# Joining the halves of a chunk's inverse on four tiles of the array, and planned margins for the router, in a DeltaNet and mixture-of-experts kernel

## The chip, the cores and the metric

The kernel runs on one core of a Trainium2 chip. The core has five engines that work at the same time, each through its own instructions in order: TensorE (PE, matrix products), VectorE (DVE), ScalarE (ACT), GpSimd (POOL) and SyncE (SP, here only for starting DMA transfers). PE reads its operands from the on-chip memory (SBUF) and writes to eight accumulator banks (PSUM). DVE and ACT copy from there. PE's weight loads are listed apart as PEld. The metric is the device time of one execution in microseconds (us): the median of three runs before the change is 909.04 us (907.24 to 909.8).

## What is computed

Two stages, all in fp32. The first is a DeltaNet attention with batch 4, 8 heads, 768 tokens and head size 48. The second sends each of the 3072 tokens to two of eight experts.

```python
for t in range(S):                       # DeltaNet, state is B x H x 48 x 48
    kt, vt, bt = k_n[:, :, t], v[:, :, t], beta[:, :, t, None]
    y[:, :, t] = einsum('bhd,bhde->bhe', q[:, :, t], state)
    v_old = einsum('bhde,bhd->bhe', state, kt)
    state = state + bt[..., None] * einsum('bhd,bhe->bhde', kt, vt - v_old)
x = y.transpose(0, 2, 1, 3).reshape(3072, 384)
logits = x @ w_gate                      # 8 experts
noisy = logits + log1p(exp(x @ w_noise)) * noise
top2, weights = two largest of noisy, softmax over the two
out[token] += weight * (relu(x[token] @ w1[e]) @ w2[e])    # 384 -> 1024 -> 384
```

## The kernel before

**DeltaNet in chunks.** The recurrence is done in chunks of 64 tokens. A *unit* is one chunk of two batch entries with their eight heads: the two entries lie in partitions 0 to 63 and 64 to 127. Two units make a chunk of all four batch entries, and four units (two chunks) make a step `s`. There are six steps. For each step the kernel does, in this order of mention (lines 1220 to 1247):

- `products(n)` for its four units: the keys are turned by PE (`turned`, L484) and copied by ACT (L489), multiplied with themselves (`by_token`, L500), and ACT copies the diagonal blocks of 32x32 into `gd` (L529) and the block below the diagonal into `at` (L535).
- `invert(s)`: DVE inverts 32x32 triangular blocks for all units of the step at once. It transposes `gd` into `t` (L546), takes the keys' lengths with a square root that ACT works out as a logarithm and an exponential (L553, L554), scales `t` with a factor that POOL prepares (`low_d`, L582, then L589), and eliminates 30 columns one after another (L597, L601). At the end it scales (L614) and transposes twice, into `tb` (L622) and `tt` (L628).
- `within(n)`: the queries are turned as the keys are, multiplied with the keys (L500), and DVE multiplies the product with a causal mask into `qk` (L693).
- `join(n)`: each 64x64 inverse is put together from two 32x32 ones. A first product (L646) multiplies `at` with `tb`, ACT negates it into `x` (L653), a second product (L658) multiplies `x` with the lower diagonal block, and ACT copies the result into the inverse `w64` (L665). Four ACT copies place the diagonal blocks (L672). A product is eight heads times two batch entries, each a 32x32x32 matmul on its own 32x32 tile of the PE array; the trace records each as two. The first product of a unit reads the upper and writes the lower rows of both batch entries, the second the other way round. So each stands on two of the array's tiles, and the two together on four. Both products of a unit use the same PSUM bank.
- `recur(n)` and `answer(n)`: the recurrence of the unit (L731, L741, L748, L759, L771), its output, and the router's logits (L814 to L853).
- `route(s)`: some 30 small instructions for the four units: exponential (L895), rounding (L897 to L903), logarithm on ACT (L980), the two largest (L913 to L930), a count of earlier tokens on PE (L935 to L941), row numbers (`r_at`, L948), weights, and POOL's eight scatters of rows to DRAM (L325).

**A planner sets the order.** None of this is issued as written. Each piece is a job with an engine, an estimated cost, the keys it reads and writes, a PSUM bank that it opens, uses or closes, and sometimes a due time. `Jobs.order` (L84) simulates the five engines with these costs, takes for each engine the ready job that is due first, and the jobs are then issued in the order of their planned starts. A job's successor is planned to be ready when the job ends, plus `SIGNAL` (0.15 us) if it stands on another engine, plus `lands`, a delay that until now only transfers have. The hardware keeps only the order: an engine whose next instruction is not ready waits, and with it what is queued behind. Two single PSUM banks and three pairs of banks serve all jobs. Jobs of expert 0 (`early`, rows of the first steps) are marked `late` and fill what is left.

**The experts.** After DeltaNet comes `rest()`, which does the remaining rows of expert 0: two row tiles are turned (L1551), copied into `xe_r` by DVE (L1555), and multiplied (L1562 and on). Experts 1 to 7 follow, with a Strassen-like scheme of seven instead of eight block products. Weights and rows come by SP's transfers, results are added with POOL's gathers and scatters.

Of the kernel before, what the change touches and what calls it, by code (L numbers as in the profile page):

```python
# [16 lines left out]
C = 64  # L17
DP = 64
Q = 32
# [19 lines left out]
class Jobs:  # L39
# [44 lines left out]
    def order(self):  # L84
        jobs = self.jobs
        for job in reversed(jobs):
            for i in job.after:
                jobs[i].due = min(jobs[i].due, job.due - job.cost - self.SIGNAL)
        for job in jobs:
            job.key = (0, job.due) if job.late is None else (1, job.late)  # L90
        waits = [len(job.after) for job in jobs]
        then = [[] for _ in jobs]
        for job in jobs:
            for i in job.after:
                then[i].append(job.number)
# [15 lines left out]

        done = []
        while len(done) < len(jobs):
            first = {}
            best = None
            for engine in self.ENGINES:
                at = []
                for i in could[engine]:
                    start = max(free[engine], ready[i], spaced if jobs[i].apart else 0.0)
                    if jobs[i].opens:  # L120
                        which = jobs[i].opens.size, jobs[i].opens.among
                        if which not in first:
# [12 lines left out]
            could[job.engine].remove(i)  # L135
            end = free[job.engine] = start + job.cost
            if job.apart:
                spaced = start + job.apart
            if job.opens:
                size, among = job.opens.size, job.opens.among  # L140
                job.opens.at = x = first[size, among][1]
                empty[size][x] = None
                job.opens.tile = self.banks[size][x]
            if job.closes:
                empty[job.closes.size][job.closes.at] = end + self.SIGNAL
            job.start = start
            if job.moves:
                end = moved = max(moved, end) + job.moves
            done.append(job)
            for j in then[i]:  # L150
                ready[j] = max(
                    ready[j],
                    end + job.lands + (self.SIGNAL if jobs[j].engine != job.engine else 0.0),
                )
                waits[j] -= 1
                if not waits[j]:
                    could[jobs[j].engine].add(j)
        return sorted(done, key=lambda job: job.start)
# [8 lines left out]
def kernel(  # L167
# [39 lines left out]
    nc = tc.nc  # L207

    B, H, S, D = q.shape
# [6 lines left out]
    US = 2 * NU  # L216
# [59 lines left out]
    before = const.tile([128, E], FP32, name="before")  # L276
# [96 lines left out]
    def deltanet(ictx):  # L373
# [10 lines left out]
        def bank(size, ahead=False):  # L384

            if size == 2:
                return Bank(2, (0, 1) if ahead else (0, 1, 2))
            return Bank(1, (0,) if ahead else (0, 1))
# [85 lines left out]
        def halves(name, slot):  # L474
            return [(name, slot, i) for i in range(2)]

        def turned(n, name, src, size, to, to_size):

            p = bank(1, True)

            def emit():
                p_t = p.tile.rearrange("p (j t) -> p j t", t=128)
                for j in range(NP):
                    nc.tensor.transpose(p_t[:, j], src(n)[:, 2 * j : 2 * j + 2], ident)  # L484

            jobs.add(PE, 0.75, emit, reads=halves(name, n % size), opens=p)
            jobs.add(
                ACT, 0.6,
                lambda: nc.scalar.copy(  # L489
                    to(n), p.tile.rearrange("p (j t) -> p j t", t=128)  # L490
                ),
                writes=[(name + "T", n % to_size)], closes=p,
            )
# [135 lines left out]
                reads=["low_d"], writes=["tt"],  # L629
            )  # L630

        def join(n):

            i = n % US
            at, w64, x = ats(n), w64s(n), xs(n)
            tb, tt = (y[:, i * H : (i + 1) * H] for y in (tbs, tts))
            pairs = [(slice(lo, lo + Q), slice(lo + Q, lo + 2 * Q)) for lo in (0, C)]
            p = bank(1)

            def p_x():  # L640
                return p.tile.rearrange("p (z h i) -> p z h i", z=2, i=Q)

            def first():
                for h in range(H):
                    for up, dn in pairs:
                        nc.tensor.matmul(  # L646
                            p_x()[dn, 0, h], at[up, h % 2, h // 2], tb[up, h],
                            start=(h == 0), stop=(h == H - 1), skip_group_check=True,
                        )

            def negated():
                for up, dn in pairs:
                    nc.scalar.mul(x[dn], p_x()[dn, 0], -1.0)  # L653

            def second():
                for h in range(H):
                    for up, dn in pairs:
                        nc.tensor.matmul(  # L658
                            p_x()[up, 1, h], x[dn, h], w64[dn, h, Q:C],
                            start=(h == 0), stop=(h == H - 1), skip_group_check=True,  # L660
                        )

            def joined():
                for up, dn in pairs:
                    nc.scalar.copy(w64[up, :, Q:C], p_x()[up, 1])  # L665

            w, below = ("w", n % NW), [("w", n % NW, lo) for lo in (Q, C + Q)]
            for lo in range(0, 128, Q):
                rows, cols = slice(lo, lo + Q), slice(lo % C, lo % C + Q)
                jobs.add(  # L670
                    ACT, 0.4,
                    lambda rows=rows, cols=cols: nc.scalar.copy(w64[rows, :, cols], tt[rows]),  # L672
                    reads=["tt"], writes=[("w", n % NW, lo)],
                )
            jobs.add(PE, 1.15, first, reads=["tb", ("at", n % NT_)], opens=p)
            jobs.add(ACT, 0.8, negated, writes=[("x", n % 2)], uses=p)
            jobs.add(PE, 1.15, second, reads=[("x", n % 2), *below], uses=p)
            jobs.add(ACT, 0.8, joined, writes=[w], closes=p)

        def within(n):  # L680

# [4 lines left out]
                lambda: by_token(  # L686
                    two_banks(p, C), kTs(n), lambda z, j, b: qTs(n)[z, j, rows_of[b]]
                ),
                reads=[("kT", n % NT_), ("qT", n % NQ)], opens=p,
            )  # L690
            jobs.add(
                DVE, 0.7,
# [181 lines left out]
        def route(s):  # L874
# [87 lines left out]
            def counted():  # L962
# [12 lines left out]
                ),  # L975
                writes=[("num", s % 2)],
            )
            jobs.add(ACT, 0.5, small_exp, reads=every_logit, writes=["r_u"])
            jobs.add(DVE, 1.0, rounding, reads=["r_u"], writes=["r_w", "r_d", "r_noisy"])
            jobs.add(ACT, 0.25, lambda: nc.scalar.activation(w, w, ACTF.Ln), writes=["r_w"])  # L980
            jobs.add(
                DVE, 0.9, noisy_logits, reads=["r_d", "noise", *every_logit],
# [4 lines left out]
            )  # L987
            jobs.add(
                DVE, 1.7, the_second, reads=["r_noisy", "r_hit0", "r_top0"],
                writes=["r_rest", "r_hit1", "r_p1", "r_taken"],  # L990
            )
            jobs.add(PE, 1.5, count_earlier, reads=["r_taken", "before"], opens=p)
            jobs.add(ACT, 0.25, lambda: nc.scalar.activation(p1, p1, ACTF.Exp), writes=["r_p1"])
            jobs.add(
                DVE, 1.5, rows, reads=["r_hit0", "r_hit1"],
# [224 lines left out]
        for s in range(NS):  # L1220
# [17 lines left out]
            for n in units:  # L1238
                load(n, "q")
                load(n, "v")  # L1240
                within(n)
            for n in units:
                join(n)
            for n in units:
                recur(n)
                answer(n)
# [29 lines left out]
    with ExitStack() as ectx:  # L1276
# [253 lines left out]
        def rest():  # L1530
# [15 lines left out]
            for i, size in enumerate(rows_in[t0:]):  # L1546
# [3 lines left out]
                for do in range(KT):  # L1550
# [1 line left out]
                        p_xt[:, do, 0:size], xr[0:size, i, do * 128 : (do + 1) * 128],  # L1552
                        ident[0:size, 0:size],
                    )
                nc.vector.tensor_copy(  # L1555
                    xe_r[:, :, i * 128 : i * 128 + size], p_xt[:, :, 0:size]
                )
            banks = [*bank_a, *bank_c, *bank_d]
# [219 lines left out]
```

## Time and profile before

The profiled execution has a span of 925.4 us; the three timed runs lie some 16 us below it. The kernel's DeltaNet part ends at about 381 us, expert 0 fills PE to 463 us, and the rest is experts 1 to 7.

| | busy us | share |
|---|---|---|
| PE | 824.5 | 89% |
| DVE | 509.0 | 55% |
| ACT | 310.2 | 34% |
| POOL | 323.7 | 35% |

| group | recorded instructions | busy us |
|---|---|---|
| L646, first product of the join | 768 | 22.4 |
| L658, second product of the join | 768 | 25.3 |
| L672, ACT copies of diagonal blocks | 96 | 38.5 |
| L653 and L665, ACT, around the products | 48 and 48 | 18.0 and 17.4 |
| L693, DVE, masked product | 24 | 16.4 |
| L980, ACT, the router's logarithm | 6 | 1.4 |
| L1555, DVE, rows of `rest()` | 2 | 0.9 |

Busy time is what the instructions of a group took, with overlapping ones counted once. A wait is charged to the instruction that could not start, and to the one that released it; everything behind it on the same engine waits too. A matmul's recorded duration holds its way through the array, so the throughput of many is read from their starts and not from one duration. PE's clock is granted at full or at half speed by stretches, and the page's slices and the rows of a stage show the mean.

### The profile page before, as it was taken

Reading aid. Unit: us, or ns where it says so; the run is one execution under the profiler, and the core shown is the slowest. Engines: PE = TensorE matmul, PEld = TensorE weight load, DVE = VectorE, ACT = ScalarE, POOL = GpSimd, SP = SyncE. Lnnn points to the kernel's source line nnn. Section 1 sums busy time; section 2 is a strip of 40 time slices with the busy share of each in tenths; the row PEclk is TensorE's granted clock in tenths of the full one; section 3 lists DMA queues with packets and bytes.
Section 4 is the critical chain, followed back from the end, with each engine's and each line's share of the span. In section 5 each row is a group of like instructions: output and inputs, shape, how many; then the busy total and the mean of one; then the engine's idle time right before and its main releaser. Section 6 shows DMA issues by size and latency. Waiting matters only on the chain. (4 is left out here: it accounts for less than half of the span.)

```text
span 925.4 us, 21745 instructions
## 1 busy us (share of the span) xinstructions
PE 824.5 (89%) x9170; PEld 639.0 (69%) x9170; DVE 509.0 (55%) x1212; ACT 310.2 (34%) x741; POOL 323.7 (35%) x331
## 2 busy tenths in 40 slices
PE   4678896989879868998899999999999999999995
PEld 3467885867758757655658758759669568578584
DVE  6959888497586971202555435455365354344342
ACT  3564635636348233311133042041140330330410
POOL 3021243332424322132441552552642624615302
PEclk8557686585775955999899999999999999999998
DMA  4698545362413122340441422414314421401201
GB/s 70 117 313 166 101 104 164 89 206 43 134 70 71 55 77 66 141 139 25 158 151 69 142 87 86 160 51 142 129 38 146 134 68 44 129 1 43 65 18 39
DMA packets 119084, 93.76 MB, mean 101 GB/s; under 512 B 84646, under 2 KB 109255, under 8 KB 118976
## 3 DMA queue, kind: packets, MB, share of 16 engines
q1 hardware_dynamic: 107312, 64.54, 25.4%
q0 software_dynamic: 9552, 27.33, 8.7%
q8 instruction: 74, 1.21, 0.6%
q10 hardware_dynamic: 2112, 0.39, 0.3%
q14 instruction: 34, 0.28, 0.1%
HBM read 58.82 MB, written 34.81 MB: 101 GB/s over the span
## 5 line engine op out<-in xcount | busy, mean ns | idle before, releaser
L367 POOL DMA_INDIRECT out_dram<-sums,index x49 | 48.5, 989 | 161.7 <-DVE sums L1267 138.9
L325 POOL DMA_INDIRECT rows_x<-y,slot x48 | 47.3, 986 | 123.5 <-DVE t L601 46.8
L597 DVE TENSOR_TENSOR part<-t 128x30 f32<-128x30 f32 (+9 forms) x180 | 69.1, 384 | 5.3
L1379 PE MATMUL a<-xe,w1e 128*128 128x416 f32 x168 | 69.2, 521 | 0.0
L601 DVE TENSOR_TENSOR t<-t,part 128x30 f32<-128x30 f32 (+9 forms) x180 | 62.9, 349 | 6.2
L358 POOL DMA_INDIRECT sums<-out_dram,index x49 | 51.6, 1054 | 34.3 <-issue 24.9
L1449 ACT COPY part_c<-c 128x416 f32<-128x416 f32 x28 | 14.1, 505 | 120.9 <-PE c L1379 120.6
L484 PE MATMUL single<-ident,kp 128*128 128x128 f32 x96 | 23.3, 388 | 34.0 <-ACT kT L489 16.8
L1379 PEld LDWEIGHTS a<-xe,w1e 128*128 128x128 f32 x168 | 29.6, 189 | 31.4 <-issue 19.2
L784 POOL COPY wide<-st 64x384 f32<-64x384 f32 x44 | 28.6, 651 | 61.4 <-DVE st L771 51.6
L1440 DVE TENSOR_TENSOR hT<-part,d 128x416 f32<-128x416 f32 x28 | 16.4, 587 | 57.8 <-ACT part L1457 56.3
L741 PE MATMUL single<-v,w 64*64 64x48 f32 x768 | 41.5, 278 | 6.1 <-issue 4.0
L1267 DVE SCALAR_TENSOR_TENSOR sums<-d,gate,sums 128x192 f32<-128x192 f32 x56 | 23.4, 417 | 42.4 <-PE d L1379 42.4
L1434 ACT ACTIVATE hT<-hT 128x416 f32<-128x416 f32 x84 | 45.1, 550 | 4.2 <-DVE hT L1440 1.4
L741 PEld LDWEIGHTS single<-v,w 64*64 64x64 f32 x768 | 38.6, 195 | 7.2 <-issue 6.8
L1416 ACT COPY xe<-x 128x384 f32<-128x384 f32 x21 | 10.0, 478 | 100.1 <-PE x L1411 100.1
L484 PEld LDWEIGHTS single<-ident,kp 128*128 128x128 f32 x96 | 15.2, 196 | 39.3 <-issue 16.6
L1379 PE MATMUL d<-xe,w1e 128*128 128x416 f32 x112 | 41.6, 513 | 0.0
L1379 PE MATMUL c<-xe,s_w 128*128 128x416 f32 x112 | 41.4, 512 | 0.0
L1440 DVE TENSOR_TENSOR hT<-part,c 128x416 f32<-128x416 f32 x28 | 16.4, 587 | 41.9 <-ACT part L1468 37.5
L672 ACT COPY w<-tt 32x256 f32<-32x256 f32 x96 | 38.5, 401 | 2.4 <-DVE tt L628 0.7
L1379 PE MATMUL d<-t_w,hT 128*128 128x192 f32 x224 | 38.6, 326 | 0.0
(242 smaller groups left out, 1917.5 us busy)
## 6 DMA issues: line engine op xcount, KB each, us to landing
w1e<-in_moe_w_dram SPq DMA_DIRECT2D x8, 1536.0 KB
w2e<-in_moe_w_dram SPq DMA_DIRECT2D x8, 1536.0 KB
xr<-rows_x SPq DMA_DIRECT2D x7, 1164.0 KB
rows_x<-empty SPq DMA_DIRECT2D x8, 776.0 KB
v<-in_v_dram SPq DMA_DIRECT2D x48, 96.0 KB
qp<-in_q_dram SPq DMA_DIRECT2D x48, 96.0 KB
out_dram<-empty SPq DMA_DIRECT2D x4, 1152.0 KB
kp<-in_k_dram SPq DMA_DIRECT2D x44, 96.0 KB
```

The source lines that it names most:

```text
L325: d = nc.gpsimd.indirect_dma_start(out=rows_x, out_offset=bass.IndirectOffsetOnAxis(ap=slot, axis=0), in_=rows, in_offset=None,).ins
L358: nc.gpsimd.indirect_dma_start(out=got, out_offset=None, in_=out, in_offset=bass.IndirectOffsetOnAxis(ap=index, axis=0), bounds_check=N - ...
L367: nc.gpsimd.indirect_dma_start(out=out, out_offset=bass.IndirectOffsetOnAxis(ap=index, axis=0), in_=got, in_offset=None, bounds_check=N - ...
L484: nc.tensor.transpose(p_t[:, j], src(n)[:, 2 * j : 2 * j + 2], ident)
L597: v_.tensor_tensor(out=part, in0=t_inv[:, j + 1 :, j, None].to_broadcast(shape), in1=t_inv[:, None, j, 0:j].to_broadcast(shape), op=ALU.mult,)
L601: latest["column"] = v_.tensor_tensor(out=t_inv[:, j + 1 :, 0:j], in0=t_inv[:, j + 1 :, 0:j], in1=part, op=ALU.add).ins
L672: lambda rows=rows, cols=cols: nc.scalar.copy(w64[rows, :, cols], tt[rows]),
L741: nc.tensor.matmul(per_head(p_u)[b, h], w64[b, h], v_n[b, h], start=(h == 0), stop=(h == H - 1), skip_group_check=True,)
L784: nc.gpsimd.tensor_copy(wide[rows, :, :, y * D : (y + 1) * D], new[rows])
L1379: nc.tensor.matmul(p, lhsT, rhs, start=opens and i == 0, stop=i == len(products) - 1, skip_group_check=True,)
L1434: relu = lambda m, l, src: nc.scalar.activation(hT[:, m, half[l]], src, ACTF.Relu)
L1440: nc.vector.tensor_tensor(out=hT[:, m, half[l]], in0=x, in1=y, op=ALU.add)
```

## The change

1. `join` takes all units of a step. The four ACT copies of each unit come first in the list. Then there are five blocks of products instead of eight: the first product of unit 0 alone; the second product of unit 0 and the first of unit 1, issued in turn, matmul by matmul; the same for units 1 and 2, and for units 2 and 3; and the second product of unit 3 alone. A mixed block stands on four 32x32 tiles, and its two results lie in the same PSUM bank, in different quarters of the partitions. Each block opens a bank of its own; it is planned at 1.25 us, where each of the eight was planned at 1.15. A block waits for all that its two products read. The number of matmuls and of ACT copies is the same.
2. In the planner, `lands` counts only for successors on another engine.
3. Jobs of compute engines get a `lands`: 2.0 us for the query product whose result DVE masks, and, in all steps but the last, 4.0 for the router's rounding, 4.0 for its second largest, 2.0 for its count.
4. In `rest()` the two copies into `xe_r` are done by ACT.

```diff
-                    end + job.lands + (self.SIGNAL if jobs[j].engine != job.engine else 0.0),
+                    end + (self.SIGNAL + job.lands if jobs[j].engine != job.engine else 0.0),
...
+            for n, m in zip([*units, None], [None, *units]):
+                p = bank(1)
+                reads = []
+                if n is not None:
+                    reads += ["tb", ("at", n % NT_)]
+                if m is not None:
+                    reads += [("x", m % 2), *(("w", m % NW, lo) for lo in (Q, C + Q))]
...
+                def products_of(n=n, m=m, p_x=p_x):
+                    for h in range(H):
+                        for up, dn in pairs:
+                            if n is not None:
+                                nc.tensor.matmul(
+                                    p_x()[dn, h], ats(n)[up, h % 2, h // 2],
+                                    part_of(tbs, n)[up, h], start=(h == 0),
+                                    stop=(h == H - 1), skip_group_check=True,
+                                )
+                            if m is not None:
+                                nc.tensor.matmul(
+                                    p_x()[up, h], xs(m)[dn, h], w64s(m)[dn, h, Q:C],
+                                    start=(h == 0), stop=(h == H - 1),
+                                    skip_group_check=True,
+                                )
...
+                jobs.add(PE, 1.25, products_of, reads=reads, opens=p)
+                if n is not None:
+                    jobs.add(
+                        ACT, 0.8, negated, writes=[("x", n % 2)],
+                        **{"closes" if m is None else "uses": p},
+                    )
+                if m is not None:
+                    jobs.add(ACT, 0.8, joined, writes=[("w", m % NW)], closes=p)
...
-                reads=[("kT", n % NT_), ("qT", n % NQ)], opens=p,
+                reads=[("kT", n % NT_), ("qT", n % NQ)], opens=p, lands=2.0,
...
+            easy = lambda x: x if paced else 0.0
...
+                DVE, 1.0, rounding, reads=["r_u"], writes=["r_w", "r_d", "r_noisy"],
+                lands=easy(4.0),
...
+                writes=["r_rest", "r_hit1", "r_p1", "r_taken"], lands=easy(4.0),
...
+                PE, 1.5, count_earlier, reads=["r_taken", "before"], opens=p, lands=easy(2.0)
...
-            for n in units:
-                join(n)
+            join(list(units))
...
-                nc.vector.tensor_copy(
+                nc.scalar.copy(
                     xe_r[:, :, i * 128 : i * 128 + size], p_xt[:, :, 0:size]
                 )
```

More of the change, by code (lines that the diff above doesn't have):

```diff
@@ L484, in emit @@
                     nc.tensor.transpose(p_t[:, j], src(n)[:, 2 * j : 2 * j + 2], ident)
-            jobs.add(PE, 0.75, emit, reads=halves(name, n % size), opens=p)
+            jobs.add(
+                PE, 0.75, emit, reads=halves(name, n % size), opens=p,
+            )
             jobs.add(
@@ L630, in invert, with join @@
             )
[L632 to L636, printed above, removed]
+        def join(units):
             pairs = [(slice(lo, lo + Q), slice(lo + Q, lo + 2 * Q)) for lo in (0, C)]
[L638 to L644, printed above, removed]
-                    for up, dn in pairs:
[L646 to L656, printed above, removed]
-                    for up, dn in pairs:
[L658 to L678, printed above, removed]
@@ new lines, in part_of @@
+            def part_of(t, n):
+                i = n % US
+                return t[:, i * H : (i + 1) * H]
+            for n in units:
+                w64, tt = w64s(n), part_of(tts, n)
+                for lo in range(0, 128, Q):
+                    rows, cols = slice(lo, lo + Q), slice(lo % C, lo % C + Q)
+                    jobs.add(
+                        ACT, 0.4,
+                        lambda rows=rows, cols=cols, w64=w64, tt=tt: nc.scalar.copy(
+                            w64[rows, :, cols], tt[rows]
+                        ),
+                        reads=["tt"], writes=[("w", n % NW, lo)],
+                    )
@@ new lines, in join, with p_x, negated, joined @@
+            for n, m in zip([*units, None], [None, *units]):
[5 more added lines that the diff above has]
+                    reads += [("x", m % 2), *(("w", m % NW, lo) for lo in (Q, C + Q))]
+                def p_x(p=p):
+                    return p.tile[:, 0 : H * Q].rearrange("p (h i) -> p h i", i=Q)
+                def products_of(n=n, m=m, p_x=p_x):
[12 more added lines that the diff above has]
+                                    skip_group_check=True,
+                                )
+                def negated(n=n, p_x=p_x):
+                    for up, dn in pairs:
+                        nc.scalar.mul(xs(n)[dn], p_x()[dn], -1.0)
+                def joined(m=m, p_x=p_x):
+                    for up, dn in pairs:
+                        nc.scalar.copy(w64s(m)[up, :, Q:C], p_x()[up])
+                jobs.add(PE, 1.25, products_of, reads=reads, opens=p)
+                if n is not None:
+                    jobs.add(
+                        ACT, 0.8, negated, writes=[("x", n % 2)],
+                        **{"closes" if m is None else "uses": p},
+                    )
+                if m is not None:
+                    jobs.add(ACT, 0.8, joined, writes=[("w", m % NW)], closes=p)
@@ L977, in route @@
             )
-            jobs.add(ACT, 0.5, small_exp, reads=every_logit, writes=["r_u"])
-            jobs.add(DVE, 1.0, rounding, reads=["r_u"], writes=["r_w", "r_d", "r_noisy"])
+            easy = lambda x: x if paced else 0.0
+            jobs.add(
+                ACT, 0.5, small_exp, reads=every_logit, writes=["r_u"]
+            )
+            jobs.add(
+                DVE, 1.0, rounding, reads=["r_u"], writes=["r_w", "r_d", "r_noisy"],
+                lands=easy(4.0),
+            )
             jobs.add(ACT, 0.25, lambda: nc.scalar.activation(w, w, ACTF.Ln), writes=["r_w"])
@@ L989, in route @@
                 DVE, 1.7, the_second, reads=["r_noisy", "r_hit0", "r_top0"],
-                writes=["r_rest", "r_hit1", "r_p1", "r_taken"],
+                writes=["r_rest", "r_hit1", "r_p1", "r_taken"], lands=easy(4.0),
             )
-            jobs.add(PE, 1.5, count_earlier, reads=["r_taken", "before"], opens=p)
+            jobs.add(
+                PE, 1.5, count_earlier, reads=["r_taken", "before"], opens=p, lands=easy(2.0)
+            )
             jobs.add(ACT, 0.25, lambda: nc.scalar.activation(p1, p1, ACTF.Exp), writes=["r_p1"])
```

## The prediction

> **What bounds the kernel now.** I read the profile page's slices first, then the time cut at the six points where DeltaNet's triangular inverse is finished on VectorE (L614), then the waits and timelines of single engines.
>
> ```profile
> span 925.4 us, 21745 instructions
> PE   4678896989879868998899999999999999999995
> PEclk8557686585775955999899999999999999999998
> 155.10:216.30 61.20, 53.42 (x1194) 46.72 (x1186) 45.40 (x122) 32.51 (x87) 19.80 (x25) 0.67 0.45 121
> 216.30:277.80 61.50, 50.70 (x1163) 44.83 (x1164) 45.48 (x123) 30.61 (x80) 19.75 (x23) 0.69 0.31 91
> 277.80:333.80 56.00, 47.10 (x1132) 41.58 (x1131) 45.02 (x124) 27.37 (x71) 20.88 (x25) 0.74 0.28 74
> 333.80:436.00 102.20, 92.37 (x1073) 66.52 (x1073) 23.02 (x78) 29.12 (x83) 22.37 (x26) 0.84 0.25 88
> 436.00:441.00 5.00, 0.88 (x6) 0.57 (x6) 4.79 (x19) 0.00 (x0) 4.62 (x3) 0.78 0.10 37
> 441.00:925.00 484.00, 467.52 (x2131) 341.61 (x2131) 221.52 (x402) 113.48 (x225) 195.78 (x159) 0.99 0.28 91
> ```
>
> Columns of the stage rows: stretch, its length, busy PE, PEld, DVE, ACT, POOL, granted clock. From 441 us on TensorE is nearly gapless at full clock, and the change touches none of it. Before that there are six periods of about 60 us. None of the engines is full: PE 47 to 53 us, DVE 45. Each period is a loop: DVE inverts, PE and ACT join the inverse's halves and run the recurrence, and DVE starts again between their requests. So DVE's idle stretches and PE's waits both matter. After 334 us only PE counts.
>
> ```profile
> 224.38 0.18 DVE L550 TENSOR_SCALAR root<-ss 128x32 f32<-128x32 f32 x1
> 235.08 0.35 DVE L559 RECIPROCAL norm<-root 128x32 f32<-128x32 f32 x1 [5.26 <-ACT root L554]
> 243.75 0.69 DVE L693 TENSOR_TENSOR qk<-pair,mask 128x512 f32<-128x512 f32 x1 [1.86 <-PE pair L500]
> DVE r_at L886 <- PE single L941: 4.6, 5, 1.9
> 268.70 0.23 ACT L980 ACTIVATE r_w<-r_w 128x32 f32<-128x32 f32 x1 [5.79 <-DVE r_noisy L902]
> ACT r_w L980 <- DVE r_noisy L902: 18.7, 5, 5.9
> PE single L484 <- ACT kT L489: 16.8, 10, 5.2
> 436.20 0.88 PE L1551 MATMUL x<-ident,xr 128*128 128x128 f32 x6 [0.66 <-DVE counts L1301]
> 441.04 4.21 PE L1562 MATMUL a<-xe_r,w1e 128*128 128x192 f32 x12 [3.97 <-DVE xe_r L1555]
> ```
>
> These come from timelines (start, duration, in brackets the idle time and its releaser) and waits up to 345 us (total, times, longest). DVE asks for a square root at 224.6 and gets it at 235.1, because ACT is deep in the join and its queue. ACT in turn stands 5.8 us before the router's logarithm (L980), and the copy of the next transposed keys (L489), queued behind it, follows at once at 268.83. PE waits 16.8 us in all for such copies.
>
> **What the Trainium skill says.** "TensorE: Matmul & The Clock Gate", section "Architectural detail: the array is 16× 32×32, not 1× 128×128": ACT and DVE are strict FIFO. The L980 row agrees: a ready copy waits behind it. "TensorEngine Tiling (Array Packing)", section "Key Properties": different tiles load weights and multiply in parallel. The trace agrees for two tiles against four (below). The first page, "Wait — 56ns, not 53.3ns?", has matmul starts never closer than about 25 ns; here L759 starts 32 matmuls on four 64x64 tiles in 0.68 us, 15 ns apart once the last one's drain is taken off, so the measurement decides. Its section "The two states you'll see": an idle window of about 3.4 us halves the clock. The trace agrees: granted clock 0.50 in 439:445 after the 3.97 us wait, 1.00 in 446:452.
>
> **The change, part by part.** All sums are against this execution's span of 925.4 us; the three timed runs have a median of 909.0, 16 us less, so I carry over differences.
>
> ```profile
> 294.28 1.92 PE L646 MATMUL single<-tb,at 32*32 32x32 f32 x64
> 296.12 1.96 PE L759 MATMUL pair<-u,kp 64*64 64x48 f32 x64
> 97.94 1.20 PE L646 MATMUL single<-tb,at 32*32 32x32 f32 x64
> 190.51 0.68 PE L759 MATMUL pair<-u,kp 64*64 64x48 f32 x32
> ```
>
> (1) The join. Now each unit has two blocks of 32 recorded matmuls (16 products) on two 32x32 tiles. At half clock (294.28) 64 of them start within 1.92 − 0.24 = 1.68 us, 26.7 ns each; at full clock (97.94) about 16 ns. After, four units take five blocks: 32, three times 64, 32; the 64 stand on four tiles. Instruction count and copies don't change. Lower bound: 26.7 ns is a floor of issue, and 64 still cost 1.68 us: nothing saved. Upper: tiles are independent, 13.3 ns, 0.85 us. I take 16 ns, the spacing seen at full clock: 1.0 us, so 0.65 saved in each of three blocks, 1.9 us a period. But ACT's join work stays: per unit four copies of 0.40, two negations of 0.375, two copies of 0.36, 3.1 us, so 12.3 a period, and it paces the stretch 221 to 229 us. Only part of PE's 5 × 1.9 us reaches DVE's wait for the root (9.1 us in three periods up to 345 us): I take 3. The last period's join lies where PE alone counts: 2 more. Sum 5; bounds −22 (rival B below) and +15 (six periods, three blocks, 0.83 each). The bank of a unit is held for about 3 us per block, not for some 8 per pair of units, which others on the two single banks can only like.
>
> (2) The margin of 2.0 for the masked product (L693) moves that DVE job 2 us later in the plan, behind columns of the inverse. DVE's waits there that stop columns or the keys' scaling are 0.77, 1.48, 1.86 and 1.49, 5.6 us; others (3.2, 2.6, 3.8) were followed by work that wasn't ready either. I take 3, bounds 0 and 5.6. Its pair bank is held longer; PE's wait for such a bank is 0.5 us in all.
>
> (3) The router's margins. The count's readers move by 2: r_at's five waits, 4.6 us, all inside the inverse; I take 3, bounds 0 and 4.6. The logarithm moves by 4: of ACT's 18.7 us of waiting, what counts is only where the next inverse was late for its input. That is once: at 169.25 after 5.8 us of idle DVE, until ACT's last copy ended at 169.22. I take 2, bounds 0 and 5. The count itself, 4 later, unblocks PE (1.7 us of waits), hidden by PE's idle time in that stretch. Queued behind the moved pieces are DVE's own router steps and POOL's row scatters; no margin for the last chunk, and the scatters of the others wait for columns anyway: nothing.
>
> (4) A margin no longer counts for a successor on the same engine: for SP that is the empty job behind the clearing; nothing, since the first scatter that waits for it starts at 121.7 us.
>
> (5) xe_r's two copies go from DVE to ACT. DVE does five weight sums first (436.52 to 439.6), so the copies come at 440.18. ACT is idle there (its next work is relu of this very product). It can copy from 437.1: 0.48 us for 128x384 on ACT (L1416's row), about 0.3 for the half. PE starts at about 437.7 instead of 441.04: 3.3 us. And without a gap over 3 us the clock should stay up: 441.04 to 445.66 at half, half of 4.6 is 2.3. PE is gapless afterwards, so both reach the end: 5.5, bounds 3 and 6.
>
> Sum: attention 5 + 3 + 5 = 13. Waits overlap and a new order makes others (PE has 4.8 us of unexplained issue gaps up to 345 us alone), so I count 8 of it. 8 + 5.5 = 13.5 us: 925.4 becomes 912, the timed median 895.5.
>
> **Rivals.** (A) Only (5) pays: the join is bound by ACT, four tiles issue no faster at half clock, and what DVE wins from its margins it waits for at L559. For it: ACT 16 of 20 us busy in 220:240. Against: r_at's waits lie within the columns, with no ACT behind. 909 − 5.5 = 903.5.
> (B) Slower: the chain of five blocks opens gaps. Each block needs the negation of the one before: 0.75 us on ACT plus two hand-offs of about 0.2, 1.15 us in which PE stands unless other work is planned there. Four gaps in six periods: 27 us. Today's two rounds cost little (waits of L658 for x and w, 4.7 us up to 345 us), as two units alternate. With no gap filled, 27 − 4.7 − 5.5 = +17: 926. It decides once more than about (4.7 + 5.5) / 27, four gaps in ten, stand open and the margins bring nothing. Against it: four transposes and four masked products a period, 0.7 to 0.8 us each, are there to fill.
> (C) It doesn't do what it says: a gain of (5) eaten by a new order, 909.
>
> **How the numbers follow.** Forecast 0.55, own range 886 to 903; A 0.20, about 900 to 906; C 0.08; B 0.17, 912 to 926. What a measurement can tell from no change is about 0.3%, 2.7 us. Faster 0.75, same 0.08, slower 0.17. The range 882 to 915 leaves out some 0.05 below (all upper bounds together are 36 us, 873; most would have to be met to pass 882) and 0.12 of B above.
>
> **What would show it.** A join of 64 within about 1.0 us at half clock (right) or 1.7 (wrong); L559's wait of 5.3 us and L693's inside the columns shrunk; r_at without wait; L980's total far below 19; the wait before L1562 under 1 us and the clock at 1.00 there; L614's period under 60 us. The prediction is wrong if L658 and L646 now wait for x for more than 10 us, if issue gaps grow, or if an earlier inverse only waits longer for the root.

## The result, and the profile after

The changed kernel takes 894.8 us (median of 4 runs, 894.5 to 896.5); the kernel before, run beside it, 909.4 (907.2 to 912.2). The ratio is 0.984, with a 95% interval of 0.981 to 0.987. The forecast was 895.5.

One thing about the baseline has to be said first. The same kernel before took a median of 925.0 us in the runs on one chip of this study (called the first below) and 908.5 to 908.7 in those on another (the second). Its profile in the prediction (span 925.4) resembles the first, its timed runs the second. So I compare two profiles that were both taken on the second chip: one more of the changed kernel (span 892.5) and one more of the kernel before (span 908.0). Ratios are always against the kernel before on the same chip.

From the page of the first profile after:

```profile
span 892.8 us, 21764 instructions
PE   4569697697968879999999999999999999999995
PEclk8657687776976879999999999999999999999998
```

The stages of the second one, cut where the inverse's last scaling begins (L616 now), then at the start and the end of the work on `rest()`'s rows of expert 0. The prediction cuts at the same points, though it says that the inverse is finished there: the scaling itself takes another 1.2 us. Columns: stretch, length, busy PE, PEld, DVE, ACT, POOL, granted clock, DMA share, GB/s.

```profile
145.80:200.20 54.40, 43.38 (x1092) 38.65 (x1093) 44.74 (x122) 26.55 (x69) 17.48 (x22) 0.73 0.49 126
200.20:265.90 65.70, 51.94 (x1286) 44.05 (x1285) 49.20 (x141) 40.33 (x104) 25.46 (x32) 0.75 0.40 111
265.90:311.30 45.40, 40.81 (x1053) 36.98 (x1053) 41.33 (x108) 22.70 (x60) 14.63 (x18) 0.73 0.21 56
311.30:408.50 97.20, 88.16 (x1156) 62.41 (x1155) 28.33 (x101) 31.14 (x88) 27.76 (x34) 0.93 0.30 103
408.50:430.60 22.10, 20.29 (x108) 14.54 (x108) 15.27 (x34) 4.30 (x12) 14.70 (x9) 1.00 0.58 192
430.60:892.50 461.90, 445.85 (x2032) 325.38 (x2030) 209.76 (x383) 109.88 (x215) 185.80 (x152) 0.99 0.27 86
```

The same stages of the kernel before on the same chip:

```profile
156.10:214.20 58.10, 51.02 (x1191) 44.93 (x1186) 44.96 (x121) 32.70 (x86) 19.78 (x25) 0.68 0.49 127
214.20:274.00 59.80, 49.11 (x1163) 43.73 (x1164) 45.63 (x122) 30.61 (x81) 19.76 (x23) 0.70 0.32 93
274.00:328.00 54.00, 45.20 (x1132) 39.66 (x1132) 45.35 (x124) 27.51 (x71) 21.00 (x25) 0.78 0.30 76
328.00:419.20 91.20, 85.65 (x1073) 60.84 (x1073) 22.79 (x77) 29.13 (x83) 22.37 (x26) 0.92 0.29 98
419.20:446.40 27.20, 21.99 (x108) 16.25 (x108) 16.21 (x36) 3.60 (x10) 14.69 (x9) 0.94 0.47 155
446.40:908.00 461.60, 445.85 (x2032) 325.40 (x2030) 209.25 (x383) 109.83 (x215) 184.99 (x152) 0.99 0.27 87
```

Read the left ends. The last inverse reaches its scaling at 311.3 instead of 328.0: 16.7 us earlier. The stretch after it grows from 91.2 to 97.2 and gives 6.0 back. The expert rows of `rest()` take 5.1 less, at clock 1.00 instead of 0.94. The experts take the same to 0.3 us. Sum: −16.7 + 6.0 − 5.1 + 0.3 = −15.5, the difference of the two spans. In the stretch that grew PE has 83 more recorded matmuls to do (1156 against 1073), work that used to stand before the last inverse: 2.5 us more of busy PE, and 3.5 more of idle.

The periods are uneven: 54.4, then 65.7, then 45.4. The long one in the middle turned out to be the key to the whole case.

### The profile page after: what moved, and what is told of

The parts are those of the page before. It is cut to its first block, busy times and chain, and to the rows that moved or that the text cites. A ratio compares the mean times of both kernels' runs of the same rounds, so it can differ in the third digit from the quotient of the medians.

```text
span 892.8 us, 21764 instructions
## 1 busy us (share of the span) xinstructions
PE 790.1 (88%) x9170; PEld 607.4 (68%) x9170; DVE 504.7 (57%) x1210; ACT 311.5 (35%) x743; POOL 321.2 (36%) x331
## 5 line engine op out<-in xcount | busy, mean ns | idle before, releaser
L325 POOL DMA_INDIRECT rows_x<-y,slot x48 | 49.1, 1023 | 109.8 <-DVE t L603 20.0
L599 DVE TENSOR_TENSOR part<-t 128x30 f32<-128x30 f32 (+9 forms) x180 | 61.9, 344 | 5.4
L1478 ACT COPY part_c<-c 128x416 f32<-128x416 f32 x28 | 14.2, 506 | 120.8 <-PE c L1408 120.8
L804 POOL COPY wide<-st 64x384 f32<-64x384 f32 x44 | 24.1, 547 | 54.4 <-DVE st L791 30.5
L761 PE MATMUL single<-v,w 64*64 64x48 f32 x768 | 38.3, 269 | 5.3 <-issue 4.0
L761 PEld LDWEIGHTS single<-v,w 64*64 64x64 f32 x768 | 36.3, 187 | 6.4 <-issue 6.2
L484 PE MATMUL single<-ident,kp 128*128 128x128 f32 x96 | 20.4, 350 | 22.5 <-DMA kp<-in_k_dram 13.8
L502 PE MATMUL pair<-st,kT 64*64 64x48 f32 x704 | 19.5, 265 | 21.3 <-DVE st L791 14.0
```

Source lines behind the costliest of these rows:

```text
L325: d = nc.gpsimd.indirect_dma_start(out=rows_x, out_offset=bass.IndirectOffsetOnAxis(ap=slot, axis=0), in_=rows, in_offset=None,).ins
L599: v_.tensor_tensor(out=part, in0=t_inv[:, j + 1 :, j, None].to_broadcast(shape), in1=t_inv[:, None, j, 0:j].to_broadcast(shape), op=ALU.mult,)
L761: nc.tensor.matmul(per_head(p_u)[b, h], w64[b, h], v_n[b, h], start=(h == 0), stop=(h == H - 1), skip_group_check=True,)
L804: nc.gpsimd.tensor_copy(wide[rows, :, :, y * D : (y + 1) * D], new[rows])
```

## The experiments

The first question was what each part is worth: alone, and taken out of the whole. Theory T was the prediction's sum (join 5, masked product 3, router 5, `xe_r` 5.5, less what overlaps); its rivals A, B and C are those of the prediction.

**The copies of `xe_r` alone.** The kernel before, with this edit:

```diff
-                nc.vector.tensor_copy(
+                nc.scalar.copy(
                     xe_r[:, :, i * 128 : i * 128 + size], p_xt[:, :, 0:size]
```

> The kernel before with part 5 alone: xe_r copied by ACT. My step says PE's wait before the first product of rest() falls from 4.0 us to under 1 and the clock stays at full there, so 5.5 us less than before (about 903.5), bounds 3 to 6. The rival that the wait is taken up later (experts 1 to 7 bound by transfers or gathers) says 0 to 2 us. In the rest of the trace nothing should differ.

Ratio 0.994 with a 95% interval of [0.992, 0.996], which is 5.6 us of 925.0. The timeline of PE at the start of `rest()`, in brackets the idle time before the instruction and what ended it:

```profile
433.83 0.88 PE L1551 MATMUL x<-ident,xr 128*128 128x128 f32 x6 [0.66 <-DVE counts L1301]
435.16 2.22 PE L1562 MATMUL a<-xe_r,w1e 128*128 128x192 f32 x12 [0.46 <-ACT xe_r L1555]
```

The wait before L1562 is 0.46 us where it was 3.97, and twelve products take 2.22 us where they took 4.21: the clock stayed up. Both halves of the step hold.

**The join alone** (the kernel before with the new `join`, and no margins):

> The kernel before with part 1 alone (five blocks of the join, two of them on four tiles). My step says 5 us less than before (about 904), of which 2 in the last step. If four tiles work fully in parallel (a mixed block of 64 in 0.84 us, as the trace of after shows), PE has 15 us less to do and the gain may reach 8. The rival that ACT paces the join says 2 us or less. The rival that a new order of the plan decides more than the PE time says anything between 10 us less and 5 us more, with the waits elsewhere than at the join.

Ratio 1.008 [1.005, 1.010]: 7 us slower, which is outside all that the expectation allowed for. (Three of the five blocks stand on four tiles, not two as it says.) The last period, between the fifth and the sixth inverse, has 77.2 us. I come back to the reason.

**The margins alone** (the changed kernel with the old `join` and the copies on DVE):

> The kernel before with parts 2 to 4 alone (margins for the masked product and for the router; join and xe_r as before). My steps say 8 us less before the discount, 5 after it (about 904). The rival that DVE loses at the root what it wins at the margins says 0 to 2 us. L980's waits on ACT must shrink in either case, from 19 us to a few.

Ratio 0.993 [0.991, 0.995], 6.8 us faster. Alone, the three are worth −5.6, +7 and −6.8; they sum to −5.4. The whole change brings −14.2 on the other chip, and a variant of it below brings −8.5 on this one. So the parts don't add.

**The same five blocks, not in turn.** Plan, banks and waits as in the changed kernel; only a mixed block's order of issue differs:

```diff
-                    for h in range(H):
-                        for up, dn in pairs:
-                            if n is not None:
+                    if n is not None:
+                        for h in range(H):
+                            for up, dn in pairs:
...
-                            if m is not None:
+                    if m is not None:
+                        for h in range(H):
+                            for up, dn in pairs:
```

> The kernel after, with the same jobs, banks, costs and so the same order, but in a mixed block the 32 matmuls of the one product are issued ahead of the 32 of the other instead of in turn. If it is the four tiles that pay, a block takes 1.68 us again at half clock instead of 0.84, 18 such blocks make up to 15 us more PE time, and by my sum a third of it and all of the last step's reaches the end: 5 to 7 us slower than after (900 to 902). If the plan's order is what pays, it is within 1 us of after (895). If the array takes the second product up before the first has ended, a block lies between 0.84 and 1.68.

Ratio 0.991 [0.989, 0.993], beside 0.984 for the change in turn (on the other chip): about 6 us of the gain need the turn, if the ratio of the changed kernel is the same on both chips; it was not timed on this one. PE's timeline of one mixed block, which PE runs at half clock:

```profile
284.99 0.90 PE L671 MATMUL single<-tb,at 32*32 32x32 f32 x26
285.67 0.26 PE L679 MATMUL single<-w,x 32*32 32x32 f32 x2
285.71 0.24 PE L671 MATMUL single<-tb,at 32*32 32x32 f32 x2
...
285.85 0.88 PE L679 MATMUL single<-w,x 32*32 32x32 f32 x26
```

The first line starts 26 matmuls in 0.90 − 0.24 = 0.66 us, some 26 ns each, on two tiles. In the middle a few of both products alternate, and then the other two tiles do their 26. The block's starts take about 1.50 us (285.85 + 0.88 − 0.24 − 284.99). In turn, on the changed kernel:

```profile
273.46 0.26 PE L671 MATMUL single<-tb,at 32*32 32x32 f32 x1
...
274.29 0.24 PE L671 MATMUL single<-tb,at 32*32 32x32 f32 x1
274.30 0.24 PE L677 MATMUL single<-w,x 32*32 32x32 f32 x1
```

The first and the last starts are 0.84 us apart, 13.3 ns each for 64. So whether four tiles are used at once is set here by the order in which the matmuls are issued; that four tiles are free isn't enough.

**The parts taken out of the whole.** On the second chip, the changed kernel itself, then with the old `join`, then without the router's margins (`easy = lambda x: 0.0`), then without the 2.0 of the masked product:

> The changed kernel, unaltered, on the chip of the runs beside it. Ratio to before 0.984 as first timed if chips don't matter to it (13 to 15 us less), within 0.980 to 0.988.

> The changed kernel with the old join (parts 2 to 5 stay). If the parts add up as measured alone (xe_r -5.6, margins -6.8), it is 12 us under before, ratio 0.987, and the join is worth only 2 us in after. If the join alone being 7 us slower was an accident of its order (a burst of scatters that starved PE), the join is worth more than that in after. My step had 5 us for it: ratio 0.990. If the join is a loss of itself, this kernel is faster than after by some us: ratio 0.977.

> The changed kernel without the router's margins (4, 4 and 2 us set to 0). My step: 5 us of gain before the discount, so 3 to 5 us slower than after. The rival that ACT's wait at the logarithm is hidden: 0 to 1. The router's pieces then cluster again and the scatters start sooner; if the bursts of scatters matter, PE's gaps inside blocks of small matmuls grow from 29 us (after) by more than 3 us.

> The changed kernel without the margin of 2 us for the masked product. My step: 3 us slower than after, and DVE's waits at the masked product come back (23 us in before, under 1 in after up to 345 us). The rival that DVE has time there: within 1 us.

| kernel | ratio [95%] | worth of the part, of 908.7 us |
|---|---|---|
| changed kernel | 0.984 [0.982, 0.987] | |
| old join | 0.990 [0.987, 0.992] | 4.6 us |
| no router margins | 0.998 [0.996, 0.999] | 11.9 us |
| no margin for the masked product | 0.985 [0.983, 0.988] | 0.9 us, within the intervals |

The worth is the difference to the first row times 908.7. The router's margins are the largest part, more than twice what I gave them. The masked product's is not to be told from nothing. Its waits did come back without the margin, in part: 5.8 us in six waits up to 345 us, against 0.7 in one with it. (The 23 us in that expectation are those of the whole run before; up to 345 us they were 12.9 in that profile.)

What do they do? Without them the last period is 73.2 us, nearly as long as in the kernel with the join alone (77.2). In both, the next inverse starts late. DVE's timeline without the router's margins:

```profile
264.51 1.94 DVE L630 STREAM_TRANSPOSE tt<-low_d 128x1024 f32<-128x1024 f32 x1
...
286.72 0.56 DVE L791 TENSOR_TENSOR st<-pair,st 128x384 f32<-128x384 f32 x1 [14.71 <-PE pair L779]
287.29 1.96 DVE L548 STREAM_TRANSPOSE t<-gd 128x1024 f32<-128x1024 f32 x1
```

L630 ends one inverse, L548 begins the next, and 22.8 us lie between their starts. The waits' view would blame the recurrence (L779), the last thing DVE waited for. But L548 needs `gd`, and these are PE and ACT of the same kernel:

```profile
283.06 2.02 PE L502 MATMUL pair<-kT 64*64 64x64 f32 x62
284.27 2.99 ACT L531 COPY gd<-pair 32x256 f32<-32x256 f32 x8 [0.41 <-PE pair L502]
```

Of the next step's four key products (L502) the last two, 64 recorded matmuls, were done only after two mixed blocks and the first products of the recurrence (L761). Their copies end at 284.27 + 2.99 = 287.26, and L548 starts at 287.29. So the inverse waited for the key products, which stood late in PE's order. In the kernel with the join alone the same pair of lines reads 295.89 + 2.98 = 298.87 for the copies, and 298.91 for the transpose.

**The key products first.** If this is the cause, then a due time for the key products of the last step must give back what the router's margins give, without them. The edit is one line, on the kernel without router margins (the planner hands a due time on to the jobs that the products need, so their inputs move forward too):

```diff
+                due=170.0 if s == 5 else None,
```

> The changed kernel without the router's margins, with one due time added: in the last step the key products of all four units are planned ahead of the join of the step before (without it two of them stand behind the first solve). The order is the same up to there. The theory: what the router's margins are worth in after is mostly the place of these key products, since the last inverse can't begin before them. Then the last period falls from 73 us to 50 or less, and since the work of expert 0 that filled the hole moves to the end, the total falls by 6 to 12 us: ratio to before 0.985 to 0.991, against 0.9975 without it. The rival (ACT's waits at the logarithm in all steps are what costs): 0.996 to 0.999.

Ratio 0.985 [0.982, 0.988]: 11.4 of the 11.9 us are back. The same two lines of DVE:

```profile
260.49 1.93 DVE L631 STREAM_TRANSPOSE tt<-low_d 128x1024 f32<-128x1024 f32 x1
262.28 1.87 DVE L549 STREAM_TRANSPOSE t<-gd 128x1024 f32<-128x1024 f32 x1
```

And ACT's copies of `gd`:

```profile
257.54 2.98 ACT L532 COPY gd<-pair 32x256 f32<-32x256 f32 x8 [0.44 <-PE pair L502]
```

Now `gd` is there before the old inverse ends, and the next one follows at once. The period has 54.2 us, 19.0 less (the expectation had 50 or less). The stretch after the last inverse grows from 89.4 to 99.7 us, so that 7.4 us remain between these two profiles; the medians are 10.7 apart.

**The same for every step.** The changed kernel still has the long period of 65.7 us, and the same mark in it:

```profile
203.33 1.96 DVE L630 STREAM_TRANSPOSE tt<-low_d 128x1024 f32<-128x1024 f32 x1
219.95 0.38 PE L502 MATMUL pair<-kT 64*64 64x64 f32 x4 [0.84 <-ACT at L537]
222.67 1.94 DVE L548 STREAM_TRANSPOSE t<-gd 128x1024 f32<-128x1024 f32 x1 [2.35 <-ACT gd L531]
```

One unit's key product starts on PE as late as 219.95 (the view ends at 220 and shows its first four matmuls), and here DVE's own wait names `gd`. So all steps from the third on get a due time, in the full change:

```diff
+                due=s * PACE - 58.0 if s > 1 else None,
```

> The changed kernel with the key products of every step but the first two due 58 us earlier than the planner's own dues would ask, so that all four stand ahead of the join of the step before in every step. In after that fails in one step: its fourth key product stands behind the second solve, and that period takes 65 us instead of 45 to 56. If the place of the key products sets when an inverse can begin, this period falls to 55 or less and the total by 3 to 8 us under after (ratio to before 0.976 to 0.981). If PE bounds the sum of the periods and the tail, or the new order costs as much elsewhere, it is within 3 us of after.

884.75 us, ratio 0.974 [0.972, 0.977]: 9 us less than the changed kernel, more than the 3 to 8 that were expected, and the best of this study. L549 now starts at 202.94, right behind L631 at 200.68. The stages:

```profile
196.60:249.90 53.30, 43.54 (x1207) 38.80 (x1206) 46.86 (x123) 33.44 (x92) 20.68 (x26) 0.79 0.40 111
249.90:303.70 53.80, 40.07 (x1040) 35.54 (x1044) 47.10 (x130) 22.84 (x60) 18.94 (x25) 0.72 0.25 62
303.70:399.20 95.50, 89.72 (x1158) 63.87 (x1151) 27.37 (x101) 31.05 (x88) 25.69 (x31) 0.92 0.31 107
```

The period of 65.7 is 53.3. The next grew from 45.4 to 53.8, but the two together fell from 111.1 to 107.1. The period before them (52.0) and the stretch after them gained 2.4 and 1.7 more. So a late start is not lost in full: DVE does other work in it, which is then missing from the next period.

**Only the logarithm's margin.** The rival explanation of the router's worth is my own: the rounding's 4.0 keeps ACT from standing before L1008. The changed kernel keeps that margin and loses the two others:

```diff
-                writes=["r_rest", "r_hit1", "r_p1", "r_taken"], lands=easy(4.0),
+                writes=["r_rest", "r_hit1", "r_p1", "r_taken"],
...
-                PE, 1.5, count_earlier, reads=["r_taken", "before"], opens=p, lands=easy(2.0)
+                PE, 1.5, count_earlier, reads=["r_taken", "before"], opens=p
```

> The changed kernel with only the first of the router's three margins (4 us ahead of the logarithm on ACT), the other two set to 0. My prediction had 2 us for this one and 3 for the count's. If it is the unblocked ACT that counts, it is within 2 us of after (ratio 0.984 to 0.987). If it is the order of the key products, it depends on the order alone: here all of the last step's stand behind the join or between its blocks, three of four ahead of the first solve, so the last period is 55 us or more and the ratio 0.988 to 0.995.

Ratio 0.996 [0.995, 0.998]: 10.9 us lost against the changed kernel. ACT's wait, up to 345 us (total, times, longest), in this kernel:

```profile
ACT r_w L1008 <- DVE r_noisy L922: 4.6, 1, 4.6
```

And with one due time and no router margins:

```profile
ACT r_w L1009 <- DVE r_noisy L923: 8.5, 3, 5.7
```

The first kernel waits less and is slower by 10 us (905.4 against 895.1). And its last period has the late start again:

```profile
258.49 1.90 DVE L630 STREAM_TRANSPOSE tt<-low_d 128x1024 f32<-128x1024 f32 x1
281.39 1.94 DVE L548 STREAM_TRANSPOSE t<-gd 128x1024 f32<-128x1024 f32 x1 [1.84 <-ACT gd L531]
```

So ACT's wait before the logarithm isn't what costs. Nor is `r_at`'s wait behind the count, the prediction's other reason: with one due time and no router margins it is longer than in the changed kernel (5.8 us against 3.9), at the same time.

```profile
DVE r_at L907 <- PE single L962: 3.3, 3, 1.2
DVE r_at L907 <- ACT r_p L1024: 2.5, 1, 2.5
```

This run also answers a rival for the late starts. In two of the kernels that have one in the last period, PE stood between the two transposes without a releaser, beside POOL's row scatters: 2.8 us without the router's margins, 5.8 with the join alone. With the logarithm's margin alone the start is as late, and such gaps come to 0.5 us. So a late start doesn't need them; they may lengthen it.

The late starts side by side, each from the end of an inverse's last transpose to the start of the next inverse's first (all on the second chip, in us):

| kernel | fourth inverse | fifth | sixth | median time |
|---|---|---|---|---|
| before | 7.6 | 0.7 | 0.8 | 908.3 |
| changed | 4.9 | 17.4 | none | 894.5 |
| no router margins | 1.6 | 6.0 | 20.8 | 905.8 |
| no router margins, due time in the last step | 0.8 | 6.0 | none | 895.1 |
| due times in all steps from the third | 0.3 | 0.3 | none | 884.8 |
| only the logarithm's margin | 5.6 | 3.9 | 21.0 | 905.4 |

The change itself brought a late start of 17.4 us that the kernel before doesn't have.

**The kernel before once more**, as the control of this set and for the stages in the section on the result:

> The kernel before, unaltered, for a profile on the chip of these runs: ratio 1.000 within 0.003. Stages and order as in the first profile; what differs between chips shows in the stages up to the experts, since the experts took 461.5 to 462.0 us in every profile so far.

Ratio 1.000 [0.998, 1.002].

## Why the prediction was right, and where it wasn't

The time was met to 0.7 us. The sum behind it was met only in two of its terms; the others missed in opposite directions.

**The join (5 us).** Worth 4.6 when taken out of the whole. The block of 64 was taken at 1.0 us at half clock and measured 0.84, the prediction's upper bound, at which each of four tiles keeps the pace that each of two had. The Trainium skill's page "TensorEngine Tiling (Array Packing)", section "Key Properties", has different tiles work in parallel; the trace agrees when neighbours in the order stand on different tiles (0.84 us) and much less so when they don't (1.50). The prediction's own lines did not show four tiles ahead of two: at full clock they have 15 ns for L759 on four larger tiles and 16 for L646 on two, and at half clock 1.96 and 1.92 us for 64. But the step took 5 as a property of the join. It isn't one: with the old margins the join costs 7 us, so that 4.6 lies near my 5 is luck in part. Its own blocks are fast there too; what changed was the planner's order, in which two key products fell behind the second mixed block and products of the recurrence. That this order is the cause there is argued from the same mark as above; the join alone was not run with a due time.

**The masked product (3 us).** Its waits did go, from 13.8 us in ten waits to one of 0.7:

```profile
DVE qk L693 <- PE pair L500: 13.8, 10, 2.7
DVE qk L713 <- PE pair L502: 0.7, 1, 0.7
```

The time hardly moved: 0.9 us, which the intervals don't tell from nothing. The failed step is the selection of "waits that stop columns": a column that starts earlier seems only to reach a later wait of DVE earlier. That link is argued, not tested.

**The router (5 us).** Mis-sized most: 11.9 us. And for another reason than the two I gave. The step said that `r_at` would lose its waits; it kept most of that time (4.7 us in five waits before, 2.5 + 1.4 in two after), and three new waits stand at `r_den`. The waits after:

```profile
DVE r_at L906 <- PE single L961: 2.5, 1, 2.5
DVE r_at L906 <- ACT w L689: 1.4, 1, 1.4
DVE r_den L975 <- ACT r_p L1023: 5.4, 3, 3.2
ACT r_w L1008 <- DVE r_noisy L922: 1.9, 1, 1.9
```

The last line is the logarithm's, L980 before. It was to fall far below 19 us, and that came: 20.2 us in five waits became 1.9 in one. But the run with the logarithm's margin alone shows that this wait was not the cost. What the margins bring together is an order in which the last step's key products come in time; there a single due time brings the same. They don't bring it everywhere: the sixth inverse's late start of 20.8 us goes, the fifth's grows from 6.0 to 17.4. The logarithm's margin alone doesn't bring it, so it takes one or both of the others; why they lead the planner there I did not follow. The prediction had seen an inverse late for its input, once, at 169.25, but put it down to the logarithm's wait on ACT; what it lacked is a term for where PE's key products stand in the order. Of the signs, "`r_at` without wait" was false, "period under 60" held in four periods of five (65.7 in the other), and "L980 ≪ 19" was true without being the reason.

**The root's wait** was to shrink: 7.7 us in four waits became 6.4 in six, the longest 3.4 became 2.5. Weakly right.

**`xe_r` (5.5 us).** Right in size and in both mechanisms: 5.6 alone, 5.1 in the stages. Without the long wait the granted clock of these rows is 1.00 instead of 0.94.

**The discount of 13 to 8.** The difference in DeltaNet was 16.7 − 6.0 = 10.7 us between two profiles, and some 9 in the timed runs (14.2 to 14.6 less 5.3). The discount was named for waits that overlap. What really happened is larger on both sides: a part that costs 7 alone, one that brings 11.9, and 6 us that come back after the last inverse. That their sum lies near my 8 is luck in part.

**The rivals.** A (only `xe_r`) is excluded: `xe_r` is 5.6 of 14.2. C, a gain eaten by a new order, is excluded by the time. B, slower through gaps before each block, had the right sign for the join alone and the wrong mechanism: with the join alone as in the changed kernel PE waits 0.9 us for `x` up to 345 us. Here the changed kernel:

```profile
PE single L671 <- ACT x L685: 0.9, 1, 0.9
PE pair L502 <- DVE st L791: 15.1, 7, 5.6
```

The second line is the largest of PE's waits for DVE's state; its longest, 5.6 us, lies in the stretch after the last inverse, where PE counts alone and 6.0 us were given back. Part (4), the planner's rule for one engine, wasn't tried by itself.

## What to carry to other kernels

When a planner writes the order, a changed cost or margin acts first through the order and only then through the wait that it was meant for; so measure each part both alone and taken out of the whole, and look for the one job whose place moved. Before crediting a shorter wait, find what the next long stage needs, and follow that input back by its own tile's times, not by the last wait of the engine that starts it. For small matmuls on array tiles, issue neighbours on different tiles: having the tiles free isn't enough.

## What the hardware showed that I had not expected

- **The pace belongs to the tile.** A mixed block needs 0.84 us at half clock; at full clock (granted 1.00), in the kernel with one due time, the 64 start within 0.56 us, some 9 ns each:

```profile
265.79 0.21 PE L672 MATMUL single<-tb,at 32*32 32x32 f32 x1 [0.16 <-ACT x L686]
...
266.35 0.19 PE L678 MATMUL single<-w,x 32*32 32x32 f32 x1
```

The Trainium skill's page "TensorE: Matmul & The Clock Gate", section "Wait — 56ns, not 53.3ns?", has no starts closer than about 25 ns; the measurement decides. Counted for one tile, the recorded matmuls of the join (32x32 on a 32x32 tile) start every 53 ns at half clock, on two tiles (2 × 26.7) and on four (4 × 13.3) alike, and every 32 to 36 ns at full clock (2 × 16 and 4 × 9). All four tiles write to one PSUM bank.

- **A high busy share does not mean full clock.** In the periods shown PE is busy for 74 to 90% of the time with many small matmuls, and the mean granted clock is 0.68 to 0.79; the experts, with 97% busy, have 0.99. Which property of the small matmuls matters was not tested.
- **The two chips differ, in one part of the kernel.** 908.5 against 925.0 us for the same kernel, in two sets of runs on the one and one set on the other. The experts take 461.5 to 462.0 us in every profile; the difference lies before them, where transfers and small matmuls are dense. Why was not tested.
- **Gaps inside blocks of small matmuls.** In the run with the join alone PE stood up to 1.11 us at a time between matmuls of one block, with nothing in the trace that it waited for, while POOL started six row scatters one after another (from 280 to 286 us). It is a coincidence seen, not a cause shown.
